# Transposing the last 64 keys of every row tile in 64x64 squares, in two groups a head, in a fused attention, mixer and expert-attention kernel

## The chip, the cores and the metric

The kernel runs on 1 core of one Trainium2 chip. The metric is the device time of one execution in microseconds (us); the profile's span runs from the first to the last instruction of the same program and is a little shorter.

## The reference

Three blocks follow each other. The first is causal attention over 4 batches x 8 heads with 576 positions and head size 64, with a bias from a running sum; the second mixes positions and channels (a low-rank mixer and a feed-forward of 512 to 2048 to 512); the third is a gated attention of 4 experts, again causal, 576 positions, head size 64.

```python
scores = scale * (q @ k.T) + minimum(-(cum_i - cum_j), 0); scores = where(causal, -1e9, scores)
attn   = softmax(scores);  x = attn @ v                       # 32 heads
u      = x + (x.T @ U @ V).T;  x = u + relu(u @ w_ch1) @ w_ch2
for e in range(4):                                            # x 4 batches: 16 heads
    a = softmax(where(causal, -1e9, scale * (x@wq[e]) @ (x@wk[e]).T))
    out += gate_e * (a @ (x@wv[e]) @ wo[e])
```

## The kernel before

Both attentions go through the class `Attn`; there are 32 heads in the first (engine table `ENGA`) and 16 in the third block (`ENGG`), 48 in all. A head's 576 queries are cut into five **row tiles** t = 0 to 4 of 64, 128, 128, 128 and 128 queries; row tile t sees `WID[t]` = 64, 192, 320, 448 and 576 keys, so its causal part is t blocks of 128 keys and then **a last piece of 64 keys**. A row tile of probabilities lies in `P` with its queries on partitions up to 127 (row tile 0 on partitions 64 to 127, its other half zero). Because of the mask, the first 64 queries of a row tile see nothing of the last 64 keys: only the square of the last 64 queries by the last 64 keys holds anything.

The product with V needs the probabilities transposed. `run` goes through steps i, five a head: step i issues the scores of row tile i % 5 (`qk`, L351 and L352), the transposes of a head that is 10 steps older (`tr`), the maximum and the move of the scores into `P` (`peak`, L362, on VectorE), the exponential of the step before (`exp`, L369, on ScalarE), the copies of the transposed tiles out of PSUM into `pt` (`evac`, which calls `cp`: L76 on ScalarE, L78 on VectorE), the row sums' division (`norm`, L380 on GpSimd), one piece of the product with V (`push_pv`, L421), and other work (fillers). The order of issue on every engine is that of the program; it is written by hand. `P` has two buffers, so in step i `peak` overwrites the row tile of the same number that the older head's transposes read, and waits for them where they are not yet done. The PSUM tile `t` has two buffers, so the transposes of step i wait for the copies of step i - 2.

The table `TRP` says for each of a head's five steps r which row tile's 128-key blocks are transposed (its first number t: t transposes of 128x128, L392) and which row tiles' last pieces (from the second number up to the third, L395). Before, a step's last pieces are transposed as all 128 queries by 64 keys, so that 64 partitions of 128 columns come out, of which `evac` copies the right half. Four of the five steps have such a group: row tiles 0 and 1 in step 0, tile 2 in step 1, tile 3 in step 2, tile 4 in step 4; step 3 has the four blocks of row tile 4. `evac` makes one copy of the blocks and one of the last pieces, on the engine that the letter of the step in `ENGA` (even and odd heads) or `ENGG` names, v for VectorE and a for ScalarE.

The first attention also carries the mixer's and feed-forward's work between its steps (L226, L238, L249, L283, L297); L238 has as its last two matmuls of each sum a pair with 64 rows in place of 128.

Of the kernel before, what the change touches and what calls it, by code (L numbers as in the profile page):

```python
# [20 lines left out]
P = 128  # L21
# [8 lines left out]
I0 = [0, 64, 192, 320, 448]  # L30
WID = [64, 192, 320, 448, 576]
OFF = [0, 64, 256, 576, 1024]
# [6 lines left out]
PST = 448  # L39
# [12 lines left out]
STREAM = (((0, 0), (2, -3)), ((-1, 4),), ((0, 1),), ((0, 2), (1, -2)), ((1, -1),), ((0, 3),))  # L52
FAST = (40, 70)

ENGA = ('vaaaaa', 'aavaav')
ULA = "gvgg"
WLE = "g"

HALVES = 152
UFIRST = 161  # L60
WIDE = (7,)
ENGG = ('aaaava', 'aaaava')

GTAB = "kkkkvvvvvqqqq......."
GATE = (9, 5, 2)
OB = "avava"
XG = 0

TRP = ((1, 0, 2), (2, 2, 3), (3, 3, 4), (4, 0, 0), (0, 4, 5))
BG = (1, 1, 0, 2, 1)  # L70
ULF = "vggg"

# [1 line left out]
def cp(nc, eng, out, in_):  # L74
    if eng == "a":
        nc.scalar.activation(out=out, in_=in_, func=AF.Copy)  # L76
    else:
        nc.vector.tensor_copy(out=out, in_=in_)  # L78


def free_ap(ap, off, dims):

    return bass.AP(tensor=ap.tensor, offset=ap.offset + off, ap=[list(ap.ap[0])] + [list(d) for d in dims])
# [65 lines left out]
def fused_kernel(ctx, tc, qk, v, s, u, vv, w12, wp, out):  # L149
    nc = tc.nc  # L150
    cst = ctx.enter_context(tc.tile_pool(name="cst", bufs=1))

    ident = cst.tile([P, P], F32, name="ident")
# [162 lines left out]
    class Attn:  # L316
# [66 lines left out]
        def tr(self, n, r):  # L383

            ps = self.pst.tile([P, 512], F32, tag="t", name=f"t_{n}_{r}")
            Pn = self.P[n % 2]
            t, a, e = TRP[r]
            for kb in range(t):  # L390
                c0 = OFF[t] + P * kb
                nc.tensor.transpose(ps[:, P * kb:P * kb + P], Pn[:, c0:c0 + P], ident)  # L392
            for k in range(a, e):
                c0, x = OFF[k] + WID[k] - 64, P * (t + k - a)
                nc.tensor.transpose(ps[0:64, x:x + P], Pn[:, c0:c0 + 64], ident)  # L395
            return ps

        def evac(self, n, r, ps):
            pt = self.pt[n % 3]
            t, a, e = TRP[r]  # L400
            if t:
                cp(nc, self.engines[n % 2][r], free_ap(pt[:, :], I0[t], [[PST, t], [1, P]]), ps[:, :P * t])
            if e > a:
                cp(nc, self.engines[n % 2][r], free_ap(pt[0:64], (PST + P) * a, [[PST + P, e - a], [1, 64]]),
                   free_ap(ps[0:64], P * t + 64, [[P, e - a], [1, 64]]))

        def push_pv(self, n):

# [87 lines left out]
    with ExitStack() as cx:  # L496
# [19 lines left out]

        attn = Attn((st, psq, pst), 4, ENGA, 0.125)
        NH = B * H
# [130 lines left out]
        def use_v(t, x):  # L649
            cs = slice(THIRD * x, THIRD * x + THIRD)  # L650
            nc.scalar.activation(out=V4[:, 0, cs], in_=t, func=AF.Copy)
            yield
            nc.vector.tensor_tensor(out=V4[:, 1, cs], in0=t, in1=V4[:, 0, cs].bitcast(F32), op=OP.subtract)
# [5 lines left out]
        for x in range(S // THIRD):  # L659
            jobs.append(job(lambda raw, x=x: nc.sync.dma_start(out=raw, in_=vv[x]), THIRD, f"v{x}",  # L660
                            lambda t, x=x: use_v(t, x)))
# [246 lines left out]
    with ExitStack() as cx:  # L908
# [17 lines left out]

        attn = Attn((st, psq, pst), 4, ENGG, 1.0)

# [162 lines left out]
        for n in range(B * E):  # L1091
            b, e = divmod(n, E)
# [105 lines left out]
```

## Time and profile before

| | |
|---|---|
| median of 3 runs (lowest to highest) | 857.36 us (856.04 to 857.37) |
| the profiled execution's own time | 857.42 us |
| its span | 855.6 us |
| busy in the span: TensorE matmul / weight load / VectorE / ScalarE / GpSimd | 94% / 87% / 61% / 56% / 38% |
| mean granted TensorE clock | 0.989 |

PE stands for TensorE's matmuls and PEld for its weight loads, which overlap them; DVE is VectorE, ACT ScalarE, POOL GpSimd. A matmul's recorded duration covers its whole way through the array, and the next one starts long before it ends; so what a matmul costs in a dense stretch is the distance from its start to the next start, not its duration. In a shape such as `128*64 128x128` the first pair is rows by columns of the array that are used, the second the moving operand's partitions by columns. Times are in us from the start of the span unless marked ns.

### The profile page before, as it was taken

How to read it: one execution, taken by the hardware profiler on the slowest of the kernel's cores; microseconds unless marked ns; L12 is line 12 of the kernel's file. 1: busy time of each engine (PE TensorE's matmuls, PEld its weight loads, DVE VectorE, ACT ScalarE, POOL GpSimd, SP SyncE). 2: the span in 40 equal slices, each digit the busy share in tenths (PEclk: the TensorE clock that was granted, in tenths of full speed). 3: DMA queues.
4: the chain of work that ended last, by engine and by line, in shares of the span. 5: the costliest groups of instructions: out<-in, count | busy, mean ns of one | idle time of the engine just before them, and what ended most of it. 6: DMA issues, size and time to landing. Idle time of an engine off the chain costs nothing.

```text
span 855.6 us, 17366 instructions
## 1 busy us (share of the span) xinstructions
PE 806.9 (94%) x6068; PEld 745.5 (87%) x6068; DVE 522.5 (61%) x1547; ACT 477.9 (56%) x1439; POOL 324.5 (38%) x498
## 2 busy tenths in 40 slices
PE   3788899999999999999999999999999989999997
PEld 3566678989879789999999999999999989898875
DVE  7578687786664647655564665455446785656541
ACT  5587777786576645324433443434333566666672
POOL 5536465364453325223332343233243043232241
PEclk9899899999999999999999999999999999999999
DMA  7887678775672051201120212110000221212121
GB/s 208 218 220 206 176 185 200 197 222 155 170 190 67 29 203 51 62 25 50 50 62 20 69 51 63 38 51 25 1 1 2 43 44 28 57 50 53 52 65 62
DMA packets 37086, 79.63 MB, mean 93 GB/s; under 512 B 4808, under 2 KB 8392, under 8 KB 37000
## 3 DMA queue, kind: packets, MB, share of 16 engines
q1 hardware_dynamic: 37000, 78.53, 34.0%
q8 instruction: 48, 0.79, 0.4%
q14 instruction: 38, 0.31, 0.1%
HBM read 38.80 MB, written 8.40 MB: 55 GB/s over the span
## 4 chain that ended last, share of the span: by engine, by line
PE 75%; DVE 4%; ACT 3%; POOL 2%; issue 1%; DMA 1%; SPq 0%; POOLq 0%; DVEq 0%; ACTq 0%
PE hps L814 20%; PE facc L832 20%; PE pv L421 6%; PE qkp L1042 5%; PE t L392 4%; PE facc L297 3%; PE hps L283 3%; PE ops L1065 3%; PE vps L975 3%; PE qk L352 2%; PE qk L351 2%; PE t L395 2%; POOL P L380 2%; DVE P L362 1%; ACT pt L76 1%
## 5 line engine op out<-in xcount | busy, mean ns | idle before, releaser
L267 POOL TENSOR_TENSOR ul<-uT,uh 128x288 fp32r<-128x288 f32 x126 | 101.4, 823 | 173.6 <-ACT uh L266 150.6
L369 ACT ACTIVATE P<-P,stat 64x64 f32<-64x64 f32 (+4 forms) x240 | 133.7, 557 | 47.7 <-DVE stat L362 45.5
L362 DVE CUSTOM_DVE_ANT_0 P<-qk,mask 64x64 f32<-64x64 f32 (+4 forms) x240 | 116.3, 486 | 44.7 <-PE qk L352 28.4
L819 DVE SCALAR_TENSOR_TENSOR hl<-hps,hh 128x288 fp32r<-128x288 f32 x110 | 50.4, 458 | 150.1 <-ACT hh L818 150.1
L380 POOL TENSOR_SCALAR P<-P,stat 64x64 f32<-64x64 f32 (+4 forms) x160 | 97.1, 621 | 109.3 <-DVE stat L375 59.7
L818 ACT ACTIVATE hh<-hps 128x288 fp32r<-128x288 f32 x110 | 45.0, 409 | 147.7 <-PE hps L814 147.5
L76 ACT ACTIVATE pt<-t 64x64 f32<-64x64 f32 (+5 forms) x304 | 89.9, 336 | 49.2 <-PE t L395 43.7
L351 PE MATMUL qk<-R,L 128*128 128x288 f32 (+4 forms) x288 | 94.7, 333 | 19.6 <-DVE L L560 9.8
L814 PE MATMUL hps<-uh,wl 128*128 128x288 f32 x376 | 111.2, 296 | 0.0
L814 PE MATMUL hps<-ul,wh 128*128 128x288 f32 x376 | 111.1, 296 | 0.0
L832 PE MATMUL facc<-hh,wh 128*128 128x288 f32 x376 | 111.1, 296 | 0.0
L814 PE MATMUL hps<-uh,wh 128*128 128x288 f32 x376 | 111.0, 295 | 0.0
L832 PE MATMUL facc<-hh,wl 128*128 128x288 f32 x376 | 110.9, 295 | 0.0
L832 PE MATMUL facc<-hl,wh 128*128 128x288 f32 x376 | 110.8, 295 | 0.0
L392 PE MATMUL t<-ident,P 128*128 128x128 f32 x480 | 89.1, 284 | 14.0 <-ACT pt L76 7.6
L380 POOL TENSOR_SCALAR P<-P,stat,pt 64x64 f32<-64x64 f32 (+4 forms) x80 | 48.3, 615 | 113.6 <-DVE stat L375 34.3
L352 PE MATMUL qk<-R,L 68*128 68x288 f32 (+9 forms) x288 | 88.8, 314 | 1.0 <-DMA L<-Cd 0.4
L392 PEld LDWEIGHTS t<-ident,P 128*128 128x128 f32 x480 | 59.1, 143 | 26.4 <-issue 10.8
L351 PEld LDWEIGHTS qk<-R,L 128*128 128x128 f32 x288 | 57.1, 198 | 25.9 <-issue 11.8
L421 PE MATMUL pv<-pt,V 128*64 128x288 f32 (+4 forms) x752 | 78.1, 356 | 0.0
L190 POOL TENSOR_TENSOR wl<-c_a_w,wh 128x256 fp32r<-128x256 f32 x56 | 43.9, 784 | 79.7 <-ACT wh L187 77.1
L421 PEld LDWEIGHTS pv<-pt,V 128*64 128x64 f32 x752 | 51.1, 144 | 26.2 <-issue 6.4
(183 smaller groups left out, 2147.0 us busy)
## 6 DMA issues: line engine op xcount, KB each, us to landing
c_raw_w<-in_w_dram SPq DMA_DIRECT2D x64, 256.0 KB
uT<-in_qk_dram SPq DMA_DIRECT2D x15, 576.0 KB
L<-HI SPq DMA_DIRECT2D x28, 288.0 KB
R<-HI SPq DMA_DIRECT2D x28, 288.0 KB
V<-in_v_dram SPq DMA_DIRECT2D x16, 320.0 KB
R<-uT SPq DMA_DIRECT2D x14, 288.0 KB
L<-uT SPq DMA_DIRECT2D x14, 288.0 KB
aD<-stage SPq DMA_DIRECT2D x6, 576.0 KB
```

The costliest lines, as they stand in the source:

```text
L76: nc.scalar.activation(out=out, in_=in_, func=AF.Copy)
L267: eng.tensor_tensor(out=l_, in0=src, in1=h_.bitcast(F32), op=OP.subtract)
L351: nc.tensor.matmul(ps[:, bk, :w], lhsT=q1[:, rows], rhs=k1[:, c0:c0 + w], start=True, stop=False)
L352: nc.tensor.matmul(ps[:, bk, :w], lhsT=q2[:, rows], rhs=k2[:, c0:c0 + w], start=False, stop=True)
L362: nc.vector.tensor_tensor_reduce(out=po, in0=view, in1=mk, scale=-self.scale, scalar=3.0e38, op0=OP.add, op1=OP.min, accum_out=stat[P - M: ...
L369: nc.scalar.activation(out=po, in_=po, func=AF.Exp, scale=-1.0, bias=stat[P - M:, 0, t:t + 1], accum_out=stat[P - M:, 1, t:t + 1])
L380: nc.gpsimd.tensor_scalar(out=pv, in0=pv, scalar1=stat[r0:, 2, t:t + 1], scalar2=1.0 if gate is None else gate(t)[r0:], op0=OP.mult, op1=O ...
L392: nc.tensor.transpose(ps[:, P * kb:P * kb + P], Pn[:, c0:c0 + P], ident)
L421: nc.tensor.matmul(ps[64 * hh:64 * hh + 64, half, lo - a:e - a], lhsT=V(hh, kb), rhs=pt[:, PST * kb + lo:PST * kb + e], start=kb == 0, sto ...
L814: nc.tensor.matmul(ps, lhsT=w[:, 0, cs], rhs=x, start=i == 0, stop=i == 11)
L819: nc.vector.scalar_tensor_tensor(out=hl, in0=ps, scalar=0.0, in1=hh.bitcast(F32), op0=OP.max, op1=OP.subtract)
L832: nc.tensor.matmul(accs[c][d], lhsT=w[:, 1, cs], rhs=x, start=f == fs[0] and i == 0, stop=f == fs[-1] and i == 2)
```

## The change

The last pieces are transposed as squares of 64 queries by 64 keys: the stationary operand and the identity are taken from partitions 64 to 127 alone, and 64 partitions of 64 columns come out. The squares of row tiles 0, 1 and 2 form one group in step 0, those of 3 and 4 a second in step 3; the four blocks of row tile 4 move from step 3 to step 4. In a step the squares now come ahead of the blocks, and one copy takes a whole group. The letters of the engines are cut to five, of which those of `ENGG` differ (step 3 on VectorE, which had step 4 before).

```diff
-ENGA = ('vaaaaa', 'aavaav')
+ENGA = ('vaaaa', 'aavaa')
-ENGG = ('aaaava', 'aaaava')
+ENGG = ('aaava', 'aaava')
-TRP = ((1, 0, 2), (2, 2, 3), (3, 3, 4), (4, 0, 0), (0, 4, 5))
+TRP = ((1, 0, 3), (2, 3, 3), (3, 3, 3), (0, 3, 5), (4, 5, 5))
             t, a, e = TRP[r]
+            for k in range(a, e):
+                c0, x = OFF[k] + WID[k] - 64, P * t + 64 * (k - a)
+                nc.tensor.transpose(ps[0:64, x:x + 64], Pn[64:128, c0:c0 + 64], ident[64:128, 64:128])
             for kb in range(t):
                 c0 = OFF[t] + P * kb
                 nc.tensor.transpose(ps[:, P * kb:P * kb + P], Pn[:, c0:c0 + P], ident)
-            for k in range(a, e):
-                c0, x = OFF[k] + WID[k] - 64, P * (t + k - a)
-                nc.tensor.transpose(ps[0:64, x:x + P], Pn[:, c0:c0 + 64], ident)
...
             if e > a:
-                cp(nc, self.engines[n % 2][r], free_ap(pt[0:64], (PST + P) * a, [[PST + P, e - a], [1, 64]]),
-                   free_ap(ps[0:64], P * t + 64, [[P, e - a], [1, 64]]))
+                cp(nc, eng, free_ap(pt[0:64], (PST + P) * a, [[PST + P, e - a], [1, 64]]),
+                   ps[0:64, P * t:P * t + 64 * (e - a)])
```

In the changed program L392 is the squares and L395 the 128x128 blocks, the other way round than before.

TensorE, steps 0 and 1 of a head in the first attention, before (`t_0` is the PSUM tile of step 0, `P_114` one of the two buffers of probabilities; the last pair is the output's partitions by columns):

```order
L351 MATMUL qk_0_274<-R_1_127,L_1_125 128x64
L352 MATMUL qk_0_274<-R_1_130,L_1_128 128x64
L392 MATMUL t_0_277<-ident,P_114 128x128
L395 MATMUL t_0_277<-ident,P_114 64x128 x2
L351 MATMUL qk_1_292<-R_1_127,L_1_125 128x192
L352 MATMUL qk_1_292<-R_1_130,L_1_128 128x192
L392 MATMUL t_1_295<-ident,P_114 128x128 x2
L395 MATMUL t_1_295<-ident,P_114 64x128
```

and in the changed program:

```order
L351 MATMUL qk_0_274<-R_1_127,L_1_125 128x64
L352 MATMUL qk_0_274<-R_1_130,L_1_128 128x64
L392 MATMUL t_0_277<-ident,P_114 64x64 x3
L395 MATMUL t_0_277<-ident,P_114 128x128
L351 MATMUL qk_1_293<-R_1_127,L_1_125 128x192
L352 MATMUL qk_1_293<-R_1_130,L_1_128 128x192
L395 MATMUL t_1_296<-ident,P_114 128x128 x2
```

Step 0 has three squares ahead of its block, and step 1 (as step 2) has blocks alone.

TensorE, steps 3 and 4 of the same head, before:

```order
L352 MATMUL qk_3_329<-R_1_130,L_1_128 128x448
L392 MATMUL t_3_332<-ident,P_114 128x128 x4
L351 MATMUL qk_4_342<-R_1_127,L_1_125 128x288
L352 MATMUL qk_4_342<-R_1_130,L_1_128 128x288
L351 MATMUL qk_4_342<-R_1_127,L_1_125 128x288
L352 MATMUL qk_4_342<-R_1_130,L_1_128 128x288
L395 MATMUL t_4_347<-ident,P_114 64x128
```

and in the changed program:

```order
L352 MATMUL qk_3_326<-R_1_130,L_1_128 128x448
L392 MATMUL t_3_329<-ident,P_114 64x64 x2
L351 MATMUL qk_4_337<-R_1_127,L_1_125 128x288
L352 MATMUL qk_4_337<-R_1_130,L_1_128 128x288
L351 MATMUL qk_4_337<-R_1_127,L_1_125 128x288
L352 MATMUL qk_4_337<-R_1_130,L_1_128 128x288
L395 MATMUL t_4_342<-ident,P_114 128x128 x4
```

The four blocks of row tile 4 went one step later, behind the scores of step 4, and two squares stand in their place.

ScalarE, steps 3 and 4 of an odd head in the first attention, before:

```order
L369 ACTIVATE P_116,stat_108<-P_116,stat_108 128x320
L76 ACTIVATE pt_106<-t_3_410 128x4x128
L369 ACTIVATE P_116,stat_108<-P_116,stat_108 128x448
L76 ACTIVATE pt_106<-t_4_424 64x64
L369 ACTIVATE P_116,stat_108<-P_116,stat_108 128x576
```

and in the changed program:

```order
L369 ACTIVATE P_116,stat_108<-P_116,stat_108 128x320
L76 ACTIVATE pt_106<-t_3_405 64x2x64
L369 ACTIVATE P_116,stat_108<-P_116,stat_108 128x448
L76 ACTIVATE pt_106<-t_4_417 128x4x128
L369 ACTIVATE P_116,stat_108<-P_116,stat_108 128x576
```

The large copy of row tile 4 now comes behind the exponential of row tile 3.

## Rows read from the trace of the kernel before

**Rows 1.** Page of the profile, part 1: busy us (share of the span) and instructions.

```profile
PE 806.9 (94%) x6068; PEld 745.5 (87%) x6068; DVE 522.5 (61%) x1547; ACT 477.9 (56%) x1439; POOL 324.5 (38%) x498
```

**Rows 2.** Page, part 4: the chain that ended last, share by engine.

```profile
PE 75%; DVE 4%; ACT 3%; POOL 2%; issue 1%; DMA 1%; SPq 0%; POOLq 0%; DVEq 0%; ACTq 0%
```

**Rows 3.** Windows by stage: us, busy us (instructions) of each engine, PEclk, DMA share, GB/s.

```profile
25.00:125.00 100.00, 81.11 (x564) 62.02 (x564) 73.19 (x239) 73.65 (x244) 54.51 (x84) 0.91 0.77 201
125.00:300.00 175.00, 170.57 (x1384) 151.70 (x1382) 119.17 (x388) 121.64 (x392) 80.88 (x129) 1.00 0.58 153
...
690.00:856.00 166.00, 155.60 (x1163) 135.76 (x1161) 88.38 (x315) 102.30 (x315) 47.91 (x85) 0.99 0.19 51
```

**Rows 4.** Windows of the same stages, the matmuls and loads of L395 alone.

```profile
25.00:125.00 100.00, 14.96 (x59) 6.77 (x59) 0.91 0.77 201
125.00:300.00 175.00, 23.30 (x97) 10.71 (x97) 1.00 0.58 153
690.00:856.00 166.00, 19.27 (x80) 8.86 (x80) 0.99 0.19 51
```

**Rows 5.** Timeline of PE, a step 0: start, us, instruction, xcount merged.

```profile
150.95 0.33 PE L392 MATMUL t<-ident,P 128*128 128x128 f32 x1
151.11 0.38 PE L395 MATMUL t<-ident,P 128*64 128x128 f32 x2
151.25 0.38 PE L283 MATMUL hps<-uh,wh 128*128 128x288 f32 x1
151.47 0.29 PE L283 MATMUL hps<-ul,wh 128*128 128x288 f32 x1
```

**Rows 6.** Timeline of PE, steps 1 to 3 of the same head.

```profile
153.12 0.39 PE L392 MATMUL t<-ident,P 128*128 128x128 f32 x2
153.34 0.27 PE L395 MATMUL t<-ident,P 128*64 128x128 f32 x1
...
153.87 0.31 PE L352 MATMUL qk<-R,L 68*128 68x320 f32 x1
154.02 0.49 PE L392 MATMUL t<-ident,P 128*128 128x128 f32 x3
...
154.66 0.37 PE L352 MATMUL qk<-R,L 68*128 68x448 f32 x1
154.87 0.60 PE L392 MATMUL t<-ident,P 128*128 128x128 f32 x4
```

**Rows 7.** Timeline of PE, L238 going from 128 rows to 64 and back.

```profile
62.22 0.28 PE L238 MATMUL mt<-xh,U 128*128 128x256 f32 x1
62.34 0.28 PE L238 MATMUL mt<-xl,U 128*128 128x256 f32 x1
62.55 0.38 PE L238 MATMUL mt<-xh,U 64*128 64x256 f32 x1
62.77 0.28 PE L238 MATMUL mt<-xl,U 64*128 64x256 f32 x1
62.98 0.42 PE L351 MATMUL qk<-R,L 128*128 128x320 f32 x1
63.23 0.31 PE L352 MATMUL qk<-R,L 68*128 68x320 f32 x1
```

**Rows 8.** Timeline of PE, L238's last 64-row matmul and transposes behind it.

```profile
287.94 0.28 PE L238 MATMUL mt<-xl,U 64*128 64x256 f32 x1
288.14 0.44 PE L392 MATMUL t<-ident,P 128*128 128x128 f32 x2
```

**Rows 9.** Groups of instructions by shape: the copies of last pieces (busy us, mean ns).

```profile
L76 ACT ACTIVATE pt<-t 64x64 f32<-64x64 f32 x112 | 23.1, 206 | 1.1 <-PE t L395 1.1
L76 ACT ACTIVATE pt<-t 64x128 f32<-64x128 f32 x32 | 8.3, 260 | 0.0
L78 DVE COPY pt<-t 64x64 f32<-64x64 f32 x32 | 6.7, 208 | 3.6 <-PE t L395 3.5
```

**Rows 10.** L362 by itself, what VectorE idled for: us, times.

```profile
  PE t L395: 11.0, 12
```

More of the change, by code (lines that the diff above doesn't have):

```diff
@@ L392, in tr @@
                 nc.tensor.transpose(ps[:, P * kb:P * kb + P], Pn[:, c0:c0 + P], ident)
-            for k in range(a, e):
-                c0, x = OFF[k] + WID[k] - 64, P * (t + k - a)
-                nc.tensor.transpose(ps[0:64, x:x + P], Pn[:, c0:c0 + 64], ident)
             return ps
         def evac(self, n, r, ps):
-            pt = self.pt[n % 3]
+            pt, eng = self.pt[n % 3], self.engines[n % 2][r]
             t, a, e = TRP[r]
             if t:
-                cp(nc, self.engines[n % 2][r], free_ap(pt[:, :], I0[t], [[PST, t], [1, P]]), ps[:, :P * t])
+                cp(nc, eng, free_ap(pt[:, :], I0[t], [[PST, t], [1, P]]), ps[:, :P * t])
             if e > a:
-                cp(nc, self.engines[n % 2][r], free_ap(pt[0:64], (PST + P) * a, [[PST + P, e - a], [1, 64]]),
-                   free_ap(ps[0:64], P * t + 64, [[P, e - a], [1, 64]]))
+                cp(nc, eng, free_ap(pt[0:64], (PST + P) * a, [[PST + P, e - a], [1, 64]]),
+                   ps[0:64, P * t:P * t + 64 * (e - a)])
         def push_pv(self, n):
```

## The prediction

> **What bounds the kernel now.** I read four views, in this order. The busy shares say that TensorE has work in flight 94% of the span and its weight loader 87% [rows 1]; no other engine passes 61%. The chain of waits agrees: 75% of it is TensorE [rows 2]. An average over stages is not enough, so the windows come next. The feed-forward between about 300 and 690 us holds no transposes of this kind. The change lies in three stretches [rows 3]: the start of the first attention (25 to 125 us), its rest (125 to 300) and the second attention (690 to 856). The weight loader is busy 62%, 87% and 82% there. A busy matmul row is a poor measure, since matmuls overlap in the array, so I take the loader's share as the part of added TensorE time that reaches the end. In the first stretch VectorE and ScalarE are at 73% and 74%, TensorE is often waiting, and the granted clock is 0.91; in the other two it is 1.00 and 0.99.
>
> The 240 last pieces fall on these stretches as 59, 97 and 80 [rows 4], the other 4 before 25 us, at five a head 11.8, 19.4 and 16 heads. Weighted by the loader's shares that is 7.3 + 16.9 + 13.1 = **37.3 heads' worth of TensorE time on the path**, of 48.
>
> Last the timeline, for what a matmul costs. Two last pieces take 0.38 us where one lasts 0.27, so the second starts 0.11 behind the first [rows 5, 6]. Four blocks take 0.60, again 0.11 apart. A block followed by a last piece, which uses 64 columns of the array but all 128 rows, shows no pause: two blocks start at 153.12 and the last piece at 153.34 [rows 6]. The last pieces cost 0.11 us each, 5 x 0.11 = 0.55 us a head, and going in and out of them costs nothing.
>
> **The change, part by part.**
>
> *Fewer moving columns.* A square moves 64 columns in place of 128. No such transpose is in the trace. Time goes by moving columns: 448 take 0.21 us and 320 take 0.15 [rows 6]. At that rate 64 columns would take 0.03, which is the lower bound (a transpose of 128 columns costs twice its share, 0.11 against 0.06); the upper is 0.11, as now. I take half of today's price, 0.055. Saved: 5 x 0.055 = 0.275 us a head (bounds 0 and 0.40).
>
> *Going from 128 rows to 64 and back.* The squares use 64 rows. The kernel does this in one other place, L238, and there it is dear [rows 7]. Matmuls of 256 columns run 0.12 us apart; the first with 64 rows starts 0.21 behind the last with 128, and the second 0.22 behind the first. So entering costs 0.09 (a pause, as if the array had to empty first) and 0.10 (as if the next weight load, no longer done ahead, lay open). Leaving is the same: 0.21, then 0.25 to the next start where the same 320 columns elsewhere take 0.15 [rows 6, 7]. Into transposes, whose loads are shorter, leaving costs 0.20 - 0.12 = 0.08 to 0.09, and then 0.44 - 0.27 = 0.17 in place of 0.11, 0.06 more [rows 8].
>
> This is a rule of the Trainium skill too: TensorEngine Tiling (Array Packing), Key Properties, says that changing the tiling mode, not merely the tile, drains the engine. For rows the trace agrees, with the 0.09 us above. For columns it does not: by the Trainium skill's list of configurations on the same page 128x64 is a mode of its own, and the last pieces of before enter it with no pause.
>
> For the squares I take 0.09 + 0.03 to enter, half of a block's open load for 64 stationary columns (bounds 0 and 0.06). In step 0 they are left into a block, 0.09 + 0.06; but the block at the head of step 0 pays an open load already, 0.16 against 0.11 [rows 5], so 0.05 falls away. Step 0: 0.12 + 0.15 - 0.05 = 0.22. In step 3 they are left into score or feed-forward matmuls: 0.12 + 0.09 + 0.10 = 0.31. Both groups: **0.53 us a head**.
>
> Net 0.53 - 0.275 = 0.255 us a head of TensorE time, and 37.3 x 0.255 = **+9.5 us**. The blocks, 480 before and after, cost the same in step 4 as in step 3.
>
> *Fewer copies.* Of 144 ScalarE copies of last pieces 80 go, of 48 on VectorE 16. The ones that stay take more columns; at 0.206 us for 64 and 0.260 for 128, 192 would take 0.31 [rows 9]. ScalarE: 31.4 us now, then 32 x 0.31 + 32 x 0.26 = 18.2, so 13 us less work. Where TensorE bounds, ScalarE waits for it and this is worth nothing. In the first stretch lies 13 x 11.8 / 48 = 3.2 us; I take half, **-1.5 us** (bounds 0 and -3.2; VectorE's share is about 1 us over the whole kernel and is left out).
>
> *Later moves of scores into P.* `peak` of row tile 3 now waits for the squares of its own step (before, its row tile had been read a step earlier): 0.12 + 0.11 behind the scores, about 0.25 with the array's depth. `peak` of row tile 4 waits for four blocks in place of one last piece: 3 x 0.11 = 0.33. Behind it on VectorE stand the next step's copies and `peak`, and ScalarE's exponential and its copies wait in turn, which free the PSUM tile for TensorE. Together 0.58 us a head, at most. VectorE idles 11 us in 12 places for such reads today [rows 10], so the wait exists but is seldom last. In the first stretch it could reach 11.8 x 0.58 = 6.8 us; elsewhere VectorE has slack, under 70% busy. I take a quarter, **+1.5 us** (bounds 0 and 6.8). The product with V, two steps later, covers the later copy of row tile 4.
>
> *Sum.* The profiled execution took 857.42 us, 0.06 over the median of the runs: 857.4 + 9.5 - 1.5 + 1.5 = **866.9, say 867.0 us**. No DMA is touched.
>
> **The rivals.**
>
> *The squares are entered and left without a pause* (faster). For it: the last pieces of before change shape with none [rows 6]. Against: they keep all 128 rows, and the one place that halves the rows pays both ways [rows 7, 8]. Then only the saving stays: 37.3 x 0.275 = 10.3, and with the copies 857.4 - 10.3 - 1.5 = 845.6 us. It decides if the two groups together cost under 0.275 us a head.
>
> *The pauses fall into waits* (no change). TensorE stalls for semaphores in every attention stage, most in the first; a drain beside such a stall is free. If half of the 0.53 is hidden so, 0.265 stands against 0.275 and the time is about 857. For it: loader shares of 62 to 87%. Against: the next matmuls in line are mostly ready (13% idle loader from 125 to 300 us is spread thin).
>
> *The later `peak` becomes the chain* (slower still). If VectorE's lateness comes last in the first stretch and in the second attention, (11.8 + 16) x 0.58 = 16.1 us in place of 1.5: 881.5 us. Against: VectorE is 53% busy in the last stretch.
>
> *Every change of tile shape drains.* Then the four groups of before would pay now, two fewer would remain, and at 0.265 us each (half of the 0.53) the change would save 2 x 0.265 + 0.275 = 0.805 a head, 30 us: 827 us. The rows show 0.11 us from block to last piece, the price of a block itself [rows 6], so it has next to no chance. This is what the Trainium skill's rule (TensorEngine Tiling (Array Packing), Key Properties) would make of the change if it held for columns as for rows.
>
> **How the numbers follow.** My forecast has 0.70, no pause 0.12, hidden pauses 0.08, the late `peak` 0.09, a drain at every shape 0.01. About 0.2% (1.7 us) is what a measurement of this kernel can tell from no change. Slower: 0.70 + 0.09, less 0.01 for a forecast that comes out under 859.1; same: 0.08 + 0.01; faster: 0.13. The forecast's own bounds are wide: with 0.03 a square, no open load on entering, and the copies at their best, (0.53 - 0.06 - 0.40) x 37.3 = 2.6 and 857.4 + 2.6 - 3.2 = 857; with 0.11 a square and all waits, 857.4 + 37.3 x 0.59 + 6.8 = 886, which is unlikely as a whole. The range goes from 857, which leaves out both faster cases (0.13), to 879, which leaves out some 0.07 at the top.
>
> **What would show it.** In the profile of the changed kernel, at L392 with a 64*64 shape: squares about 0.055 us apart; a first square that starts about 0.09 later behind its scores than the columns of these need, with no weight load ahead of it; the same behind the last square. TensorE busy time hardly falls, although 240 matmuls are shorter. ScalarE has 80 instructions fewer. The feed-forward takes as long as before. VectorE's idle time for L392 and L395 together rises above 11 us. The prediction is wrong if the weight load of a square stands beside the scores' last matmul, if the squares take 0.11 us, or if the three attention stretches grow by less than 5 us in all.

## The result, and the profile after

| | before | changed |
|---|---|---|
| median of 4 runs each | 856.88 us (856.04 to 857.37) | 866.92 us (864.50 to 870.53) |
| the profiled execution's own time, and its span | 857.42, 855.6 | 868.47, 866.7 |
| mean granted TensorE clock in it | 0.989 | 0.983 |

The ratio is 1.0108, 95% interval 1.0083 to 1.0133: the change makes the kernel slower by 9 to 10 us, as forecast.

The page's busy line of the changed kernel:

```profile
PE 819.9 (95%) x6068; PEld 744.2 (86%) x6068; DVE 522.6 (60%) x1531; ACT 475.3 (55%) x1359; POOL 323.7 (37%) x498
```

Against [rows 1] the matmuls are as many and 240 of them have half the columns, yet TensorE is busy 13.0 us longer, and the span grows by 11.1. ScalarE has its 80 instructions less, but only 2.6 us less work.

Its windows over the two stretches of the first attention (columns as in [rows 3]):

```profile
25.00:125.00 100.00, 84.67 (x551) 64.27 (x550) 71.68 (x229) 71.70 (x225) 53.14 (x82) 0.88 0.78 206
125.00:300.00 175.00, 171.60 (x1364) 147.05 (x1362) 119.91 (x380) 119.76 (x359) 81.32 (x130) 1.00 0.57 149
```

In the same 100 us TensorE gets 13 matmuls fewer done, in the next 175 us 20 fewer, while its busy time rises in both. In the second stretch the granted clock is 1.00 before and after, so there the loss is not the clock's. In the first it is 0.88 against 0.91 [rows 3], a mean over times at full clock (2.4 GHz) and at half (1.2 GHz): of the delay there up to 3 us, an estimate from these two rows, may be the clock's. The kernel as a whole is not slower because of the clock. On the chip where both were timed again (the change again, below), fourteen runs of the kernel before with a granted clock of 0.987 to 0.989 took 855.75 to 861.72 us, and the four runs of the changed kernel with the same clock 864.16 to 867.27.

Followed by a head's first score matmul (heads counted from 0), the kernel is 3.3 us late at head 13 (120.55 against 117.29 us) and 5.9 at head 31 (284.55 against 278.68). It is 6.0 late at the first matmul of the feed-forward (L814, 308.08 against 302.09) and of the third block (L1042, 664.96 against 658.95), and 11.2 at the last matmul (L1065, 861.41 against 850.16). So all of it comes in the three attention stretches, and the feed-forward between them adds nothing. A second profile of the changed kernel is 5.4 late at the same two places and 8.3 at the end.

The timeline of PE in a step 0 of the changed kernel, and under it that of the weight loader in the same 0.7 us:

```profile
199.10 0.28 PE L352 MATMUL qk<-R,L 68*128 68x64 f32 x1
199.30 0.36 PE L392 MATMUL t<-ident,P 64*64 64x64 f32 x3
199.59 0.33 PE L395 MATMUL t<-ident,P 128*128 128x128 f32 x1
199.67 0.38 PE L297 MATMUL facc<-hh,wh 128*128 128x288 f32 x1
```
```profile
199.07 0.19 PEld L352 LDWEIGHTS qk<-R,L 68*128 68x128 f32 x1
199.30 0.20 PEld L392 LDWEIGHTS t<-ident,P 64*64 64x64 f32 x3
199.59 0.14 PEld L395 LDWEIGHTS t<-ident,P 128*128 128x128 f32 x1
```

The score matmul before the squares has 64 columns, and still the first square starts 0.20 behind it. In the kernel before, the block that follows the same matmul starts 0.11 behind it, at 150.95 [rows 5]:

```profile
150.84 0.28 PE L352 MATMUL qk<-R,L 68*128 68x64 f32 x1
```

The load of the first square starts at 199.30 with the square, not under the scores; the one of the block starts at 199.59 with the block. That is what it looks like when nothing is loaded ahead over a change from 128 rows to 64 and back. Taken one by one, the squares start 0.083 and 0.056 us apart and the block 0.147 behind the last: 0.056 is the price of a square, 0.027 the first square's open load, 0.09 the pause before the block.

VectorE's wait for reads of the buffer that it overwrites, in the view of L362 by itself (idle us, times):

```profile
  PE t L392: 18.4, 17
  PE t L395: 6.8, 12
```

These 25.2 us stand against 11.0 [rows 10]. The groups of L362 and L369 for row tile 3, which has 448 keys, and of L369 for row tile 4 with 576 show where (busy us, mean ns, then the idle time before them). Before:

```profile
L369 ACT ACTIVATE P<-P,stat 128x576 f32<-128x576 f32 x48 | 37.1, 774 | 13.8 <-DVE stat L362 13.8
L369 ACT ACTIVATE P<-P,stat 128x448 f32<-128x448 f32 x48 | 31.8, 662 | 2.1 <-DVE stat L362 1.9
L362 DVE CUSTOM_DVE_ANT_0 P<-qk,mask 128x448 f32<-128x448 f32 x48 | 29.5, 615 | 8.5 <-PE qk L352 8.4
```

and after:

```profile
L369 ACT ACTIVATE P<-P,stat 128x576 f32<-128x576 f32 x48 | 37.2, 774 | 6.7 <-DVE stat L362 6.4
L369 ACT ACTIVATE P<-P,stat 128x448 f32<-128x448 f32 x48 | 31.9, 664 | 10.3 <-DVE stat L362 10.1
L362 DVE CUSTOM_DVE_ANT_0 P<-qk,mask 128x448 f32<-128x448 f32 x48 | 29.6, 617 | 11.4 <-PE t L392 11.1
```

VectorE waits 11.1 us for the squares of step 3 before it overwrites row tile 3 (before, that wait was for the scores, 8.4 us), and ScalarE's exponential behind it 10.3 us where it waited 2.1. But the exponential of row tile 4 waits 6.7 in place of 13.8, so on ScalarE the wait has moved rather than grown (15.9 us for the two before, 17.0 after).

### The profile page after: what moved, and what is told of

It reads as the page before. It is cut to its first block, busy times and chain, and to the rows that moved or that the text cites. A ratio compares the mean times of both kernels' runs of the same rounds, so it can differ in the third digit from the quotient of the medians.

```text
span 866.7 us, 17086 instructions
## 1 busy us (share of the span) xinstructions
PE 819.9 (95%) x6068; PEld 744.2 (86%) x6068; DVE 522.6 (60%) x1531; ACT 475.3 (55%) x1359; POOL 323.7 (37%) x498
## 4 chain that ended last, share of the span: by engine, by line
PE 82%; DMA 4%; ACT 4%; DVE 4%; POOL 2%; issue 1%; SPq 1%; POOLq 0%; ACTq 0%; DVEq 0%
PE hps L814 20%; PE facc L832 20%; PE pv L421 7%; PE qkp L1042 6%; PE t L395 5%; PE hps L283 3%; PE facc L297 3%; PE qk L352 3%; PE qk L351 3%; PE ops L1065 3%; PE vps L975 2%; PE t L392 2%; DVE P L362 1%; DMA uT<-in_qk_dram 1%; ACT pt L76 1%
## 5 line engine op out<-in xcount | busy, mean ns | idle before, releaser
L369 ACT ACTIVATE P<-P,stat 64x64 f32<-64x64 f32 (+4 forms) x240 | 133.9, 558 | 48.3 <-DVE stat L362 45.9
L362 DVE CUSTOM_DVE_ANT_0 P<-qk,mask 64x64 f32<-64x64 f32 (+4 forms) x240 | 116.5, 487 | 55.4 <-PE qk L352 26.1
L351 PE MATMUL qk<-R,L 128*128 128x288 f32 (+4 forms) x288 | 96.8, 340 | 20.5 <-DVE L L560 9.8
L76 ACT ACTIVATE pt<-t 128x256 f32<-128x256 f32 (+5 forms) x224 | 85.2, 397 | 53.9 <-PE t L395 51.6
L814 PE MATMUL hps<-uh,wl 128*128 128x288 f32 x376 | 111.4, 296 | 0.0
L814 PE MATMUL hps<-ul,wh 128*128 128x288 f32 x376 | 111.3, 296 | 0.0
L814 PE MATMUL hps<-uh,wh 128*128 128x288 f32 x376 | 111.1, 296 | 0.0
L395 PE MATMUL t<-ident,P 128*128 128x128 f32 x480 | 92.2, 292 | 6.8 <-ACT pt L76 4.5
L352 PE MATMUL qk<-R,L 68*128 68x288 f32 (+9 forms) x288 | 91.2, 321 | 0.9 <-DMA L<-Cd 0.4
L351 PEld LDWEIGHTS qk<-R,L 128*128 128x128 f32 x288 | 59.5, 207 | 25.7 <-issue 16.5
L395 PEld LDWEIGHTS t<-ident,P 128*128 128x128 f32 x480 | 59.6, 145 | 19.0 <-ACT pt L76 7.0
```

Of the source, the lines that this page charges most:

```text
L351: nc.tensor.matmul(ps[:, bk, :w], lhsT=q1[:, rows], rhs=k1[:, c0:c0 + w], start=True, stop=False)
L352: nc.tensor.matmul(ps[:, bk, :w], lhsT=q2[:, rows], rhs=k2[:, c0:c0 + w], start=False, stop=True)
L362: nc.vector.tensor_tensor_reduce(out=po, in0=view, in1=mk, scale=-self.scale, scalar=3.0e38, op0=OP.add, op1=OP.min, accum_out=stat[P - M: ...
L369: nc.scalar.activation(out=po, in_=po, func=AF.Exp, scale=-1.0, bias=stat[P - M:, 0, t:t + 1], accum_out=stat[P - M:, 1, t:t + 1])
L814: nc.tensor.matmul(ps, lhsT=w[:, 0, cs], rhs=x, start=i == 0, stop=i == 11)
```

## The experiments

The theory: the pauses on entering and leaving the squares cost more than their halved columns save, and the new order costs about nothing. Its rivals: the order is what costs, by the reads of `P` that it puts late; or 64 columns cost, not 64 rows. So squares and order are taken apart first.

**The order alone.** The last pieces as before (128 rows by 64 columns of the array, right half copied), all else as changed.

```diff
-  transpose(ps[0:64, x:x + 64], Pn[64:128, c0:c0 + 64], ident[64:128, 64:128])
+  transpose(ps[0:64, x:x + P], Pn[:, c0:c0 + 64], ident)
...  (x and the copy's source follow)
```

> The changed kernel's groups, order and copies, but each last piece transposed as before: all 128 query rows, 128 moving columns, the right half copied out. Theory (the pauses on going from 128 rows to 64 and back cost 0.53 us a head, the halved columns give back 0.275): no pause and no saving are left, so the time is that of the kernel before, 857 us, within 2 us (fewer copies against a later peak). Rival (the regrouping is what costs: the moves of scores into P wait longer): 867 us, as the changed kernel.

Measured: 861.16 us (856.32 to 866.06, 12 runs), ratio 1.0021 (0.9993 to 1.0049).

```profile
PE 808.6 (94%) x6068; PEld 748.1 (87%) x6068; DVE 523.0 (61%) x1531; ACT 474.1 (55%) x1359; POOL 324.3 (38%) x498
```

TensorE is busy 1.7 us more than before [rows 1], not 13.0. The squares hold most of the loss, the order 1.8 us most likely (-0.6 to +4.2).

The timeline gives what the squares of the change cost TensorE in its own order. A step 0 and a step 3 of one head, first with the order alone:

```profile
151.07 0.27 PE L352 MATMUL qk<-R,L 68*128 68x64 f32 x1
151.18 0.52 PE L392 MATMUL t<-ident,P 128*64 128x128 f32 x3
151.53 0.27 PE L395 MATMUL t<-ident,P 128*128 128x128 f32 x1
151.78 0.29 PE L283 MATMUL hps<-ul,wh 128*128 128x288 f32 x1
...
154.79 0.36 PE L352 MATMUL qk<-R,L 68*128 68x448 f32 x1
154.99 0.38 PE L392 MATMUL t<-ident,P 128*64 128x128 f32 x2
155.35 0.30 PE L283 MATMUL hps<-ul,wh 128*128 128x288 f32 x1
```

and in the changed kernel:

```profile
154.59 0.28 PE L352 MATMUL qk<-R,L 68*128 68x64 f32 x1
154.79 0.35 PE L392 MATMUL t<-ident,P 64*64 64x64 f32 x3
155.38 0.30 PE L283 MATMUL hps<-ul,wh 128*128 128x288 f32 x1
...
158.39 0.37 PE L352 MATMUL qk<-R,L 68*128 68x448 f32 x1
158.69 0.30 PE L392 MATMUL t<-ident,P 64*64 64x64 f32 x2
159.16 0.29 PE L283 MATMUL hps<-ul,wh 128*128 128x288 f32 x1
```

From the score matmul to the second matmul behind the transposes, step 0 takes 0.79 us in place of 0.71 and step 3 0.77 in place of 0.56: the squares cost 0.29 us a head.

**Squares in the order of before.** All four groups stay where they were; a piece is a 64x64 square.

```diff
-  transpose(ps[0:64, x:x + P], Pn[:, c0:c0 + 64], ident)
+  transpose(ps[0:64, x + 64:x + P], Pn[64:128, c0:c0 + 64], ident[64:128, 64:128])
```

> The kernel before with its four groups a head, its order and its copies, but each last piece transposed as a 64x64 square with 64 rows. Theory: four groups are entered and left for 0.31 us each, 1.24 us a head, less 0.275 saved: 0.965 x 37.3 heads on the path, 857 + 36 = 893 us (885 to 900). Rival (the regrouping is what costs, the squares themselves save): 847 to 857 us.

Measured: 885.16 us (882.46 to 886.87), ratio 1.0309 (1.028 to 1.0337), +26.5 us. The direction was as expected, the size lies at the low end of the 885 to 900 expected. The busy line, and the timeline of PE in the same step 2 as in [rows 6]:

```profile
PE 850.5 (96%) x6068; PEld 754.7 (85%) x6068; DVE 521.0 (59%) x1547; ACT 481.2 (55%) x1439; POOL 324.5 (37%) x498
```
```profile
153.88 0.49 PE L392 MATMUL t<-ident,P 128*128 128x128 f32 x3
154.30 0.24 PE L395 MATMUL t<-ident,P 64*64 64x64 f32 x1
154.47 0.47 PE L351 MATMUL qk<-R,L 128*128 128x448 f32 x1
154.78 0.38 PE L352 MATMUL qk<-R,L 68*128 68x448 f32 x1
155.00 0.60 PE L392 MATMUL t<-ident,P 128*128 128x128 f32 x4
```

This is the cleanest price of one group, since only the square differs. From the first block of step 2 to the first block of step 3 it takes 155.00 - 153.88 = 1.12 us, against 154.87 - 154.02 = 0.85 in [rows 6]: +0.27. My price for a group that is left into scores was 0.31, less 0.055 for the one square's columns, 0.255. But over the whole kernel TensorE's busy time rises by 43.6 us and the span by 27.1, so 0.62 of the added work reached the end. What TensorE waited for shrank: span less busy time is 48.7 us before and 32.2 here.

**64 columns of all 128 rows.** To see whether the columns drain the array too, the pieces are ordinary fp32 products with the identity's right half, in the order of the change.

```diff
-  transpose(ps[0:64, x:x + 64], Pn[64:128, c0:c0 + 64], ident[64:128, 64:128])
+  matmul(ps[0:64, x:x + 64], lhsT=Pn[:, c0:c0 + 64], rhs=ident[:, 64:128], start=True, stop=True)
```

> The changed kernel with all 128 query rows as the stationary operand's rows and the right 64 columns of the identity as the moving operand, as an ordinary fp32 matmul in place of a transpose: 64 moving columns, no change from 128 rows to 64. Theory, if only the rows matter: no pause, 5 x 0.055 us a head saved, 857 - 10 = 847 us. Rival: an ordinary matmul with 64 stationary columns is entered with a pause as the product with V is (0.20 us from the last transpose to it, in place of 0.11): about 0.5 us a head of pauses again, 865 to 868 us.

Measured: 870.48 us (869.40 to 875.26), ratio 1.0153 (1.0122 to 1.0184). The timeline of PE in a step 0:

```profile
202.09 0.27 PE L352 MATMUL qk<-R,L 68*128 68x64 f32 x1
202.29 0.56 PE L392 MATMUL t<-ident,P 128*64 128x64 f32 x6
202.78 0.33 PE L395 MATMUL t<-ident,P 128*128 128x128 f32 x1
```

The time is over even the rival's 865 to 868, and says little by itself, since each such product shows as two matmuls (x6 for three pieces, 240 more in all). But the timeline shows the rival's pause: the first one starts 0.20 behind the scores, as a square does, although all 128 rows are used. The rule of the Trainium skill (TensorEngine Tiling (Array Packing), Key Properties), that changing the tiling mode drains the engine, fits this pause of an ordinary matmul of 64 columns; for the transposes of before, which use 128 rows and 64 columns too, [rows 6] show no pause. Why the two differ no run here settles. The shape in a row tells which rows and columns are used, not which mode the array is in, so those transposes may not change the mode at all. Nor does this run tell the 64 columns apart from the product's being done as two matmuls.

**Where the second group stands, with squares.** The squares of row tiles 3 and 4 in step 2 and the blocks of row tile 4 in step 3, so that no read is late.

```diff
-TRP = ((1, 0, 3), (2, 3, 3), (3, 3, 3), (0, 3, 5), (4, 5, 5))
+TRP = ((1, 0, 3), (2, 3, 3), (3, 3, 5), (4, 5, 5), (0, 5, 5))
```

> The changed kernel with its squares in two groups, of which the second stands in step 2 behind that step's other work, and with the blocks of row tile 4 back in step 3; step 4 has no transposes. So no row tile is read in the step in which it is overwritten, but for row tile 0. Theory: the pauses stay, the later peak (which I put at 1.5 us) goes: 865 us. Rival (the later peak is what costs): 857 us or less.

Measured: 862.19 us (859.26 to 865.60, 12 runs), ratio 1.0045 (1.0024 to 1.0066): against 1.0108 and 1.0084 for the change (the second from the change again, below). So the late reads do cost, some 3 to 5 us of the change's time. In the third block the copy of the four blocks falls on VectorE here, by `ENGG`, so it isn't the place alone.

**All squares in one group,** in step 0:

```diff
-TRP = ((1, 0, 3), (2, 3, 3), (3, 3, 3), (0, 3, 5), (4, 5, 5))
+TRP = ((1, 0, 5), (2, 5, 5), (3, 5, 5), (0, 5, 5), (4, 5, 5))
```

> The changed kernel with all five squares of a head in one group, in step 0, and one copy for them; blocks of row tiles 1 to 4 in steps 0, 1, 2 and 4 as in the changed kernel. Theory (the pauses belong to the groups): one group is entered and left for 0.09 + 0.03 + 0.09 + 0.06 - 0.05 = 0.22 us a head, the halved columns give 0.275 back, so TensorE has 0.055 us a head less to do than before: 855 to 857 us, plus up to 4 us for waiting in step 0 until GpSimd has divided row tiles 3 and 4. Rival (squares or regrouping are dear by themselves): 865 us or more.

Measured: 862.80 us (858.84 to 865.71, 12 runs), ratio 1.0052 (1.0032 to 1.0072). A group less helps, by 3 to 5 us. But TensorE's busy time is no more than before, and still the kernel is slower, and slower than the 855 to 861 expected. Its busy line, its window of the first stretch, and TensorE's wait for GpSimd's division ahead of the squares (us, times, longest):

```profile
PE 806.3 (94%) x6068; PEld 744.3 (87%) x6068; DVE 518.9 (60%) x1515; ACT 473.2 (55%) x1327; POOL 324.7 (38%) x498
```
```profile
25.00:125.00 100.00, 80.27 (x552) 63.32 (x551) 71.74 (x230) 71.47 (x215) 53.57 (x83) 0.86 0.77 201
```
```profile
PE t L392 <- POOL P L380: 4.4, 9, 0.8
```

The granted clock is 0.86 there against 0.91 [rows 3], with TensorE busy about as much. Over all its runs the clock is 0.970 to 0.982, lower than in every run of before (0.986 to 0.995). At the 0.7 us for 0.001 of clock that the runs of before show (last section), a mean lower by 0.012 goes with some 8 us, more than the whole loss; this is an estimate, and whether the wait lowers the clock is not shown.

**Full rows, three groups, early blocks.** The pieces of 128 rows again; row tile 3's last piece in step 2, row tile 4's in step 4, its blocks in step 3.

```diff
-ENGG = ('aaava', 'aaava')
+ENGG = ('aaaav', 'aaaav')
-TRP = ((1, 0, 3), (2, 3, 3), (3, 3, 3), (0, 3, 5), (4, 5, 5))
+TRP = ((1, 0, 3), (2, 3, 3), (3, 3, 4), (4, 4, 4), (0, 4, 5))
...  (the transposes and copies as with the order alone)
```

> Last pieces as before (128 rows, 128 columns, no pause), in three groups: row tiles 0 to 2 in step 0, 3 in step 2, 4 in step 4, and the blocks of row tile 4 back in step 3. Against the run with the changed schedule alone it has one group and one copy a head more, and no row tile but 0 and 4 is read in the step that overwrites it. Theory (the later moves of scores into P cost some 2 us in that run): 857 us. Rival (that run's excess comes from elsewhere or is none): 860 us.

Measured: 854.32 us (852.39 to 857.23, 12 runs), ratio 0.9956 (0.9937 to 0.9975), faster than both kernels and than the 857 expected.

**The change again, and with its copies one by one** (144 more of them):

```diff
-  if e > a: cp(nc, eng, free_ap(pt[0:64], (PST + P) * a, [[PST + P, e - a], [1, 64]]), ps[0:64, P * t:P * t + 64 * (e - a)])
+  for k in range(a, e): cp(nc, eng, free_ap(pt[0:64], (PST + P) * k, [[1, 64]]), ps[0:64, P * t + 64 * (k - a):P * t + 64 * (k - a) + 64])
```

> The changed kernel itself, on the same chip as these runs: 867 us, 1.01 of the kernel before. Every theory expects this; it is the base that the other three are compared with.

> The changed kernel with each of the five squares of a head copied by itself, so 3 copies a head or 144 in all more, some 0.2 us each on ScalarE and VectorE. Theory (ScalarE and VectorE mostly wait for TensorE; 96 copies fewer were worth 1.5 us): 2 to 3 us over the changed kernel. Rival (the copies are on the path in most heads): 8 us or more over it.

Measured: 865.48 us (864.05 to 867.27), ratio 1.0084 (1.0062 to 1.0106), and 868.41 us (865.21 to 873.11), ratio 1.0122 (1.0093 to 1.0151). The difference, 0.0038 or 3.3 us, is about as large as its own uncertainty; at that rate, 0.023 us a copy, the 96 copies fewer of the change are worth 2.2 us.

**Full rows, two groups, every read early.** The full-row version with three groups, but with row tiles 3 and 4 as a second group in step 1; only row tile 0 is still read in the step that overwrites it.

```diff
-TRP = ((1, 0, 3), (2, 3, 3), (3, 3, 4), (4, 4, 4), (0, 4, 5))
+TRP = ((1, 0, 3), (2, 3, 5), (3, 5, 5), (4, 5, 5), (0, 5, 5))
```

> Last pieces as before (128 rows, 128 columns, no pause) in two groups, row tiles 0 to 2 in step 0 and 3 and 4 in step 1; blocks as in the kernel before. One group and one copy a head less than the run with three such groups, which took 0.9956 of the kernel before, and no later move of scores for row tile 4; but step 1 needs row tile 4 divided by GpSimd two steps earlier. Theory (fewer copies and earlier reads help, nothing pauses): 850 to 854 us. Rival (waits for GpSimd in step 1 take it back): 857 us or more.

Measured: 852.12 us (850.61 to 855.39), ratio 0.993 (0.9908 to 0.9953). It is the fastest version: it keeps the change's two groups and drops its squares and its late reads.

```profile
PE 802.8 (94%) x6068; PEld 747.2 (88%) x6068; DVE 519.6 (61%) x1515; ACT 475.4 (56%) x1375; POOL 326.9 (38%) x498
```

**Squares in the order with three groups:**

> The 64x64 squares of the change in the schedule of the run with three groups (row tiles 0 to 2 in step 0, 3 in step 2, 4 in step 4; blocks as before). Theory (each group is entered and left): 0.22 + 0.27 + 0.31 - 0.275 = 0.525 us a head over that run, of which the four-group run showed some 0.6 reach the end: 854 + 48 x 0.525 x 0.6 = 869 us. Rival (the schedule, not the squares, makes the loss of the changed kernel): 855 to 858 us.

Measured: 871.18 us (866.81 to 872.43, 5 runs), ratio 1.0146 (1.012 to 1.0172). The edit is that of the first experiment, backwards. Beside the full rows in the same order, 0.9956, the squares cost 0.0190, 16.3 us.

**Squares in the order with two early groups,** likewise:

> The squares of the change in the schedule of full_rows_two_groups (groups in steps 0 and 1, blocks of row tile 4 in step 3; 0.993 of before with full rows). Theory: squares cost about 10 us for each group a head and save about 14 us by their 64 columns, whatever the schedule, so two groups cost 5 to 8 us: 0.993 + 0.0075 = 1.0005 of before, within 0.998 to 1.004. Then the schedule of the change (the second group in step 3, the blocks of row tile 4 in step 4) costs the change 7 us, and its squares the rest. Rival: the waits of the change's schedule hide part of the pauses, and where these waits are absent the squares cost 10 us or more: 1.005 or above. Other rival: the schedule's cost shows only beside full rows; then this kernel is as slow as the change, 1.009.

Measured: 862.68 us (860.28 to 864.77), ratio 1.0062 (1.0041 to 1.0082).

```profile
PE 816.0 (95%) x6068; PEld 744.2 (87%) x6068; DVE 517.9 (60%) x1515; ACT 476.1 (55%) x1375; POOL 325.1 (38%) x498
```

Here the squares cost 0.0132, 11.3 us, more than I expected; this was the first rival's number. TensorE is busy 13.2 us longer than with full rows.

**Early group, late blocks.** The order alone (the first experiment), with the second group moved from step 3 to step 1 (the diff is against the changed kernel, the transposes and copies are those of the first experiment):

```diff
-TRP = ((1, 0, 3), (2, 3, 3), (3, 3, 3), (0, 3, 5), (4, 5, 5))
+TRP = ((1, 0, 3), (2, 3, 5), (3, 5, 5), (0, 5, 5), (4, 5, 5))
```

> The schedule of schedule_alone (full rows) with one thing moved: the last pieces of row tiles 3 and 4 go from step 3 to step 1, ahead of the steps that overwrite them; the four blocks of row tile 4 stay late, in step 4. It stands between schedule_alone (1.002 of before) and full_rows_two_groups (0.993), from which it differs by the place of the blocks alone. If the late blocks of row tile 4 carry the cost (0.33 of the 0.58 us that were worked out), it stays at 1.000 to 1.003; if the group in step 3, on which the maximum of row tile 3 waits, carries it, it falls to 0.993 to 0.996. The trace after the change has ScalarE's wait moved to row tile 3's exponential, which speaks for the second; I expect 0.995.

Measured: 855.92 us (854.03 to 857.61, 12 runs), ratio 0.9979 (0.9964 to 0.9994). I expected 0.995. It lies in the middle: the group in step 3 holds 0.0042 (3.6 us) and the late blocks 0.0049 (4.2 us), each uncertain by about 0.003, so each late read seems to cost something, and neither alone is the answer. The group's move also takes its copy in the third block from VectorE to ScalarE.

VectorE's idle time for such reads, in the view of L362, is 10.2 + 6.0 = 16.2 us with the order alone:

```profile
  PE t L392: 10.2, 10
  PE t L395: 6.0, 10
```

With full rows in two early groups it is only

```profile
  PE t L392: 7.6, 5
```

less than the 11.0 of before [rows 10].

## Why the prediction was right, step by step

The four corners, as ratios to before:

| | full rows | squares | squares cost |
|---|---|---|---|
| two groups, reads early | 0.993 | 1.0062 | 0.0132, 11.3 us |
| two groups, reads late (the change's order) | 1.0021 | 1.0108 and 1.0084 | 0.0063 to 0.0087, 5.4 to 7.5 us |
| late reads cost | 0.0091, 7.8 us | 0.0022 to 0.0046, 1.9 to 3.9 us | |

Each difference is uncertain by about 0.003 to 0.004. Between the two rows of the table the engine of one copy differs too: in the third block the second group is copied by VectorE with late reads and by ScalarE with early ones. In the order in which I summed (regroup, then squares, then late reads) the terms are: -6.0 us measured for -1.5; +11.3 for +9.5; +1.9 to +3.9 for +1.5. They make +7.2 to +9.2 us, where I had +9.5.

- **What bounds it: right.** The chain of the changed kernel is TensorE's by more than before [rows 2]:

```profile
PE 82%; DMA 4%; ACT 4%; DVE 4%; POOL 2%; issue 1%; SPq 1%; POOLq 0%; ACTq 0%; DVEq 0%
```

- **Fewer moving columns: right.** I took 0.055 us a square; the timeline shows 0.056.
- **From 128 rows to 64 and back: right** in kind and size. No load runs ahead, and the pauses are there on both sides. Step 0 of before takes 0.63 us (150.84 to 151.47), so 0.74 with a third last piece of 0.11; the changed kernel's 0.79 is 0.05 more, and its step 3 0.21 more than with full rows. Together that is 0.26 us a head, where I had 0.255. By an average of my two prices, two, three and four groups cost 37.3 x (0.265 n - 0.275) = 9.5, 19.4 and 29.3 us (for four, with 0.31 for each, I had put down 36); measured in orders without the change's late reads they cost 11.3, 16.3 and 26.5. The last pieces of before I took for a tile mode of 64 columns that is entered without a pause; no row shows which mode they are in.
- **The share that reaches the end: roughly right, as an average.** I took 37.3 heads of 48, or 0.78. Of TensorE's added busy time 11.3 of 13.2 us reached the end with two early groups (0.86), 0.62 with four, and in the change's own order 5.4 to 7.5 of 11.3 (0.5 to 0.7), where pauses and late reads both stop TensorE. That the two overlap is read from the table; with intervals this wide it is likely rather than settled. The split between the blocks fits: 24.2 of the weighted heads, 6.2 us, in the first attention and 13.1, 3.3 us, in the second; the two profiles of the changed kernel are 6.0 and 5.4 us late behind the first, and 5.2 and 2.9 more behind the second.
- **Fewer copies: the step that failed.** I gave two groups for four -1.5 us, at most -3.2, from 13 us less work on ScalarE. The durations of its copies of last pieces do go down so, from 31.4 to 10.0 + 8.2 = 18.2 us, but a small copy, 0.206 us, had begun some 0.10 us before the instruction ahead of it ended: all copies of L76 out of PSUM together are busy 4.7 us less. Before and after, with the after's two forms by themselves:

```profile
L76 ACT ACTIVATE pt<-t 64x64 f32<-64x64 f32 (+5 forms) x304 | 89.9, 336 | 49.2 <-PE t L395 43.7
```
```profile
L76 ACT ACTIVATE pt<-t 128x256 f32<-128x256 f32 (+5 forms) x224 | 85.2, 397 | 53.9 <-PE t L395 51.6
L76 ACT ACTIVATE pt<-t 64x192 f32<-64x192 f32 x32 | 10.0, 312 | 0.0
L76 ACT ACTIVATE pt<-t 64x128 f32<-64x128 f32 x32 | 8.2, 257 | 0.7 <-PE t L392 0.7
```

  Still, with every read early the regrouping is worth 0.0070, 6.0 us (4.0 to 7.9). By the copies that were split, 2.2 us of that are the copies. The run also reads the last piece of row tile 4 in step 1, which the kernel before reads in the step that overwrites it, and puts the pieces ahead of the block in step 0, where a third piece then adds only 0.08 us (0.71 against 0.63) in place of 0.11. How much each of these is worth isn't traced: TensorE's busy time is 4.1 us lower than before, with the same matmuls.
- **Later moves of scores into P: too small by itself, right beside the squares.** The mechanism is as described: 25.2 us of idle time on VectorE for those reads. With full rows it costs 7.8 us, just over my upper bound of 6.8; with squares 1.9 to 3.9 (3 to 5 by the version with the second group in step 2). That the sum came out within 0.1 us of the median is luck: it rests on this and the step before erring opposite ways.
- **The clock: left out.** I had no term for it. It is a little lower in the changed kernel's runs, 0.979 to 0.989 against 0.986 to 0.995. Where both ran on one chip, the medians are 7.1 us apart over all runs and 7.2 over those of equal clock, so it does not make the loss.

The rivals: *no pause* is refuted by the timeline and by every pair of squares and full rows. *The pauses fall into waits* is true in part, as the share above says, but not so far that the halved columns pay for them. *The late peak becomes the chain* is not what happened, since VectorE holds 4% of the chain as before. *Every change of tile shape drains* is not so for the transposes of before, though the ordinary matmuls of 64 columns do pause.

## What to carry to other kernels

Going into a tile of half the rows and out again costs a pause of about 0.09 us and an open weight load each way, some 0.3 us a visit; two or three halved transposes, which save 0.05 us each, don't pay for it, and five in one visit about break even (TensorE busy 806.3 us against 806.9). So read the distance from start to start at such a place before you shrink an operand. Where a buffer is read and overwritten in turn, keep the reads ahead of the step that overwrites it: the two late reads cost 7.8 us with full rows, more than the 6.0 that the grouping saves. An edit that bundles a gain with two losses should be taken apart: the grouping alone, with full rows and early reads, made the kernel 0.7% faster.

## What was not expected of the hardware

These fp32 transposes, which use 128 rows and 64 columns, start without a pause behind those that use 128 columns (0.11 us from start to start). Ordinary fp32 matmuls that use as many rows and columns start with one (0.20 us behind the scores, in place of 0.11).

The scatter between executions goes with the granted clock. Over 74 runs of the kernel before, 853.69 to 862.76 us, a clock lower by 0.001 goes with 0.7 us more; with the order alone, one run at 0.994 took 856.32 us and one at 0.982 took 866.06. So what is read as the price of an edit of a few us can hold a part that is the clock's, as in the version with one group; which of the two comes first no run here shows. The squares in two early groups, for instance, ran at 0.982 to 0.990 and their full-row partner at 0.987 to 0.994, so a part of their 11.3 us may be the clock's too.
